# A fused attention and feed-forward kernel: the product of two weights as Strassen's seven products of quarters, with weight tiles in shared places, one-engine copies of G and a new order

## Chip, cores, metric

One core of one Trainium2 chip. The metric is the device time of one execution in microseconds (us). Executions are grouped as fast or slow by the granted TensorE clock and the time, and only fast ones are compared. The chip changes from batch to batch, so every batch carries its own executions of the kernel before. A ratio is the mean time of one kernel's fast runs over the mean of the other's fast runs of the same rounds, so it is not quite the ratio of the medians quoted beside it; the bracket is its 95% interval. The granted clock is the share of TensorE's full rate that the profile shows; a spell at half clock is a stretch in which it was about 0.5. PE is TensorE, DVE VectorE, ACT ScalarE, POOL GpSimd, SP the engine that issues most loads.

## The reference, cut to what matters

```python
def _attn_ref(q, k, v):            # 8 batches, 8 heads, 576 tokens, 64 wide; 32 landmarks
    q_lm, k_lm = (mean of 18 tokens each)
    A, Bm, C = sm(q, k_lm), sm(q_lm, k_lm), sm(q_lm, k)
    Z = (scaled transpose of Bm)
    for _ in range(6):
        Z = 2 * Z - Z @ Bm @ Z
    return A @ Z @ C @ v

def _moe_ref(x, w1, w2, w3, w_out):    # x 4608 x 512; w1, w2 512 x 1024; w3 1024 x 1024; w_out 1024 x 512
    h = (x @ w1) * (x @ w2) @ w3
    return h @ w_out
```

The kernel multiplies the two last weights first: w34 = w3 w_out, in fp32, called **the fold**. It also multiplies the small Z C v with w1 and w2, which gives G, so that x @ w1 becomes A times G.

## The kernel before

A list of tokens gives the order of instructions on all engines. `f` is one product of the fold, `P`, `Q` transposes on PE, `T` a transposing DMA, `M` and `L` token sums (on DVE or POOL), `E` a copy that duplicates a part of w1 and w2 into the other 64 partitions, `G` the part of G from w1 or from w2 for four heads, `U` an up unit, `D` a down chunk, `K` a load of k or q, `W` a load of v, `l` a load of one of the sixteen halves of w3's row blocks. In the new list, `t` transposes such a half, `T1` to `T4` are sums of w_out, and small `g` is a `G` whose copy goes to DVE.

```python
ORDER = """
f f f f f f f f l l f f f l f l f f f f Pk01 f Pk02 Qk00 Qk03 Qq01 f Pq00 l Pk11 f Qk13 f Qq03 Pq02 f
# ... cut ...
U D U U D D D D D
"""

def prod(j, c):                         # the fold: 8 rows x 8 steps of 512 columns, fp32
    if c == 0:
        psw[j] = psf.tile([128, 512], FP32, name="psw", bufs=2)
    nc.tensor.matmul(psw[j], w3ts[j, c // 4][:, c % 4, :], wof[:, c, :],
                     start=(c == 0), stop=(c == 7))
    if c == 7:
        nc.scalar.copy(out=w34[:, j, :], in_=psw.pop(j))

def gproj(b, qd, w):                    # G: 8 matmuls, then one half copied by ACT, one by DVE
    # ... cut ...
    nc.scalar.activation(out=dst[:, 0], in_=psG[:, 0], func=AXF.Copy, scale=1.0 / ZS)
    nc.vector.tensor_scalar(out=dst[:, 1], in0=psG[:, 1], scalar1=1.0 / ZS, scalar2=None,
                            op0=ALU.mult)

def dup_weights(hh):
    nc.vector.tensor_copy(out=wdup[64:128, hh], in_=wdup[0:64, hh])

# the start: SP issues w3, ACT issues w_out in whole rows (five issues)
for i in range(2):
    load_w3(i, nc.sync)
load_wo(0, 1); load_wo(1, 1); load_wo(2, 2)
load_w3(2, nc.sync)
load_wo(4, 2); load_wo(6, 2)
load_w3(3, nc.sync)
```

The softmax here doesn't subtract the row's maximum and nothing guards it: scores larger than these inputs give would overflow.

## Time and profile before

| | before |
|---|---|
| time, median of 3 runs | 298.24 us (296.69 to 299.67) |
| span of the profiled run | 297.0 us, clock 0.987 |
| busy share PE, weight load, DVE, ACT, POOL | 94, 56, 57, 46, 34% |
| first up unit (the first product of ahat and G) starts | 97.2 us |
| from there to the end | 199.8 us |

The prediction below shows the lines of the page. PE is the bound. And the start of the **first up unit** divides the span: nearly all of the fold's work comes ahead of it, and it is the mark. This view of the kernel before gives busy time on both sides of that mark (columns: stretch, length, then PE, weight load, DVE, ACT, POOL busy, granted clock, DMA share, GB/s):

```profile
0.00:97.20 97.20, 91.69 (x921) 48.15 (x922) 48.32 (x106) 32.89 (x59) 36.51 (x57) 1.00 0.98 199
97.20:297.00 199.80, 188.02 (x2772) 118.18 (x2771) 120.17 (x224) 102.52 (x183) 63.38 (x95) 0.98 0.63 125
```

PE is idle 97.2 - 91.69 = 5.5 us ahead of the mark and 199.8 - 188.0 = 11.8 us behind it.

### The profile page before, as it was taken

The page shows a single profiled execution, that of the slowest core. Times are in us where ns is not written, and L with a number is a line of the kernel's source. Part 1 is how long each engine was busy: PE and PEld are TensorE (multiplying, and loading weights), DVE is VectorE, ACT ScalarE, POOL GpSimd, SP SyncE. Part 2 cuts the span into 40 slices and gives each one's busy share as a digit, 9 for nine tenths or more (in the row PEclk, how much of TensorE's full clock was granted, in tenths as well). Part 3 has the DMA queues.
Part 4 walks back from the last instruction along what each step waited for, and adds up shares of the span by engine and source line. Part 5 has one row for each costly group of instructions (what it writes and reads, how often), then busy time and mean ns, then how long its engine had stood idle before and what let it go on. Part 6 is the DMA issues. An engine that isn't in the chain of part 4 may idle for free.

```text
span 297.0 us, 8655 instructions
## 1 busy us (share of the span) xinstructions
PE 279.7 (94%) x3693; PEld 166.3 (56%) x3693; DVE 168.5 (57%) x329; ACT 135.4 (46%) x242; POOL 99.9 (34%) x151
## 2 busy tenths in 40 slices
PE   6999998999998798998899979999999999999994
PEld 2545554555643565675466746635577764566552
DVE  1701587312888868667777576757656466554320
ACT  2015444431144566334666524486565435554341
POOL 0600803640458536386935315381520200000000
PEclk9999999999999999998899998999999999999999
DMA  6999799999979997988988995736931023223234
GB/s 205 376 249 231 192 225 148 178 152 149 155 117 204 235 163 130 169 169 173 216 141 160 142 176 138 110 80 144 256 101 38 4 59 87 71 56 88 67 86 132
DMA packets 57446, 44.34 MB, mean 149 GB/s; under 512 B 30016, under 2 KB 48960, under 8 KB 57408
## 3 DMA queue, kind: packets, MB, share of 16 engines
q1 hardware_dynamic: 42560, 30.06, 45.4%
q0 software_dynamic: 13632, 11.54, 26.2%
q10 hardware_dynamic: 1216, 2.20, 2.1%
q8 instruction: 29, 0.48, 0.7%
q14 instruction: 9, 0.07, 0.1%
HBM read 38.80 MB, written 9.44 MB: 162 GB/s over the span
## 4 chain that ended last, share of the span: by engine, by line
PE 77%; DVE 8%; ACT 7%; DMA 4%; issue 2%; SPq 0%; DVEq 0%; ACTq 0%
PE psw L535 19%; PE small L458 18%; PE big L430 18%; PE small L328 4%; PE big L410 4%; PE small L279 4%; DMA qT<-nat 3%; PE pst L519 2%; PE big L300 2%; ACT gt L414 2%; DVE ab L437 2%; DVE lp L184 2%; ACT a_sb L436 1%; DMA w3f<-in_moe_w_dram 1%; PE small L321 1%
## 5 line engine op out<-in xcount | busy, mean ns | idle before, releaser
L430 PE MATMUL big<-ahat,gt 128*128 128x288 f16 x512 | 73.4, 291 | 4.4 <-DVE gt L415 1.7
L437 DVE TENSOR_TENSOR ab<-a_sb,big 128x576 f16<-128x576 f16 x64 | 48.1, 753 | 37.4 <-ACT a_sb L436 34.3
L458 PE MATMUL small<-w,ab 128*128 128x512 f16 (+1 forms) x296 | 68.0, 376 | 0.1
L535 PE MATMUL psw<-wof,w3t 128*128 128x512 f32 x128 | 64.6, 623 | 0.0
L430 PEld LDWEIGHTS <-gt 128*128 128x128 f16 x512 | 48.8, 99 | 24.9 <-issue 8.8
L436 ACT CAST a_sb<-big 128x576 f16<-128x576 f32 x64 | 40.8, 638 | 25.3 <-PE big L430 23.8
L458 PEld LDWEIGHTS <-ab 128*128 128x128 f16 x296 | 28.2, 99 | 29.8 <-issue 2.7
L462 ACT ACTIVATE o_sb<-small 128x512 f32<-128x512 f32 (+1 forms) x36 | 21.3, 591 | 47.1 <-PE small L458 42.6
L310 POOL TENSOR_TENSOR e<-ect 96x384 f32<-96x384 f32 x16 | 15.9, 996 | 53.9 <-ACT ect L305 51.0
L535 PEld LDWEIGHTS psw<-wof,w3t 128*128 128x128 f32 x128 | 22.0, 195 | 15.1 <-issue 13.6
L415 DVE TENSOR_SCALAR gt<-big 128x512 f16<-128x512 f32 x32 | 21.1, 687 | 10.8 <-ACT gt L414 10.6
L414 ACT ACTIVATE gt<-big 128x512 f16<-128x512 f32 x32 | 18.0, 596 | 9.5 <-PE big L410 9.4
L410 PE MATMUL big<-wdup,zt 128*32 128x512 f16 x256 | 18.5, 397 | 1.9 <-DVE zt L398 1.0
L190 POOL TENSOR_TENSOR ls<-qT 128x384 f32<-128x384 f16 x12 | 11.8, 982 | 24.4 <-ACT qT L134 16.7
L530 ACT COPY w3t<-pst 128x512 f32<-128x512 f32 x13 | 7.6, 586 | 22.1 <-PE pst L519 22.1
L184 DVE TENSOR_REDUCE lp<-kT 128x256 f32<-128x2304 f16 x6 | 15.3, 2548 | 1.3 <-ACT kT L134 1.2
L279 PE MATMUL small<-sz 32*32 32x64 f32 (+1 forms) x768 | 15.0, 215 | 0.6 <-DVE sz L285 0.6
L279 PEld LDWEIGHTS small<-sz 32*32 32x32 f32 x768 | 11.3, 106 | 6.6 <-issue 4.6
L305 ACT ACTIVATE ect<-big 96x768 f32<-96x768 f32 x16 | 12.9, 806 | 4.2 <-PE big L300 4.1
L328 PE MATMUL small<-vt,ect 96*32 96x64 f32 x768 | 13.8, 221 | 0.0
L380 DVE TENSOR_TENSOR ahat<-eat,big 128x576 f16<-128x576 f16 x16 | 11.8, 749 | 3.4 <-PE big L377 3.3
L285 DVE TENSOR_TENSOR sz<-sz,small 128x256 f32<-128x256 f32 x20 | 8.3, 418 | 9.1 <-PE small L279 8.8
(105 smaller groups left out, 296.8 us busy)
## 6 DMA issues: line engine op xcount, KB each, us to landing
vt<-in_v_dram SPq DMA_DIRECT2D x8, 1152.0 KB, 9.4
out_dram<-o_sb SPq DMA_DIRECT2D x23, 192.0 KB, 2.3
nat<-in_k_dram POOLq DMA_DIRECT2D x7, 576.0 KB, 10.9
nat<-in_q_dram POOLq DMA_DIRECT2D x7, 576.0 KB, 8.8
out_dram<-o_sb SPq DMA_DIRECT2D x24, 128.0 KB, 2.4
w3g<-in_moe_w_dram SPq DMA_DIRECT2D x8, 256.0 KB, 6.2
wdup<-in_moe_w_dram POOLq DMA_DIRECT2D x2, 1024.0 KB, 8.8
w3f<-in_moe_w_dram SPq DMA_DIRECT2D x7, 256.0 KB, 6.0
```

The lines of the kernel that those rows point to most:

```text
L184: nc.vector.tensor_reduce(out=lp, in_=tt.rearrange("p h j (l g) -> p h l j g", g=3), axis=AX.XY, op=ALU.add)
L279: nc.tensor.matmul(psI[sl, 64 * a:64 * a + n], src[sl, a, 32:64], src[sl, a, 0:n], start=True, stop=True, tile_position=(32 * h, 32 * h))
L328: nc.tensor.matmul(psV[32 * h:32 * h + 32, 0:64], st["ect", qd][:, c, h, :], st["v"][:, 4 * qd + h, c, :], start=(c == 0), stop=(c == TK - 1),
L410: nc.tensor.matmul(psG[32 * h:32 * h + 32, n, :], st["zt"][h % 2][:, qd, h // 2, :], wdup[:, 4 * qd + h, w, 512 * n:512 * n + 512], start= ...
L414: nc.scalar.activation(out=dst[:, 0], in_=psG[:, 0], func=AXF.Copy, scale=1.0 / ZS)
L415: nc.vector.tensor_scalar(out=dst[:, 1], in0=psG[:, 1], scalar1=1.0 / ZS, scalar2=None, op0=ALU.mult)
L430: nc.tensor.matmul(p[:, c, 0:HS], st["g", qd][:, w, 128 * j:128 * j + 128], st["ahat", qd][:, c, :], start=(qd == 0), stop=(qd == 1))
L436: nc.scalar.copy(out=a_sb, in_=p[:, :, 0:HS])
L437: nc.vector.tensor_tensor(out=ring["ab"][:, j, off:off + S].rearrange("p (c s) -> p c s", c=2), in0=a_sb, in1=pp[1][:, :, 0:HS], op=ALU.mult)
L458: nc.tensor.matmul(pso[:, f0:f1], ab[:, j, pos:pos + 128], w34[:, j, f0:f1], start=(j == 0), stop=(j == 7))
L462: nc.scalar.activation(out=o_sb[:, f0:f1], in_=pso[:, f0:f1], func=AXF.Copy, scale=1.0 / (X64 * X64))
L535: nc.tensor.matmul(psw[j], w3ts[j, c // 4][:, c % 4, :], wof[:, c, :], start=(c == 0), stop=(c == 7))
```

## The change

The intent: the fold's 64 fp32 products of 512 columns become 112 of 256 (Strassen's seven products of quarters, in the form with fifteen sums), which is 12.5% fewer columns for PE. The sums go to DVE and one in each row block to POOL. Of the sixteen halves of w3, fourteen are loaded into the places that w1 and w2 take later and two into a place of G, so no load waits for an earlier half to be used up. One engine copies a whole half of G (ACT 23, DVE 9). Token sums are issued in halves. The order of all work is new, also behind the fold.

```diff
 ORDER = """
-f f f f f f f f l l f f f l f l f f f f Pk01 f Pk02 Qk00 Qk03 Qq01 f Pq00 l Pk11 f Qk13 f Qq03 Pq02 f
+l f f t T1 f l f t T3 l f l l l f t f f f l f l f f t f f T2 f f W1 f T4 f f t f f f f f f f f t f f f f
 ... (all of the list is new)
-    def gproj(b, qd, w):
+    def gproj(b, qd, w, eng):
-        nc.scalar.activation(out=dst[:, 0], in_=psG[:, 0], func=AXF.Copy, scale=1.0 / ZS)
-        nc.vector.tensor_scalar(out=dst[:, 1], in0=psG[:, 1], scalar1=1.0 / ZS, scalar2=None,
-                                op0=ALU.mult)
+        if eng is nc.scalar:
+            nc.scalar.activation(out=dst, in_=src, func=AXF.Copy, scale=1.0 / ZS)
+        else:
+            nc.vector.tensor_scalar(out=dst, in0=src, scalar1=1.0 / ZS, scalar2=None,
+                                    op0=ALU.mult)
+    raws = [wpool.tile([128, 8, 512], FP32, name=f"raw{w}", tag=f"w{w}") for w in range(2)]
+    def wo_sum(i):
+        out, a, b = {1: (T1, B12, B11), 2: (T2, B22, T1), 3: (T3, B22, B12), 4: (T4, B21, T2)}[i]
+        nc.vector.tensor_tensor(out=out, in0=a, in1=b, op=ALU.subtract)
     def turn_w3(i):
+            nc.vector.tensor_tensor(out=s1, in0=pst, in1=tA[r, "22"], op=ALU.add)
+            nc.vector.tensor_tensor(out=s3, in0=tA[r, "11"], in1=pst, op=ALU.subtract)
+            nc.vector.tensor_tensor(out=s2, in0=s1, in1=tA[r, "11"], op=ALU.subtract)
+    PRODS = {1: ("11", B11), 2: ("12", B21), 3: (4, B22), 4: ("22", T4), 5: (1, T1), 6: (2, T2),
+             7: (3, T3)}
+    def prod(r, k, c):
+            acc[r, k] = psf.tile([128, 256], FP32, name="psw", bufs=3)
+        nc.tensor.matmul(ps_, lhs[:, 128 * c:128 * c + 128], right[:, c],
+                         start=(c == 0), stop=(c == 3))
+        elif k == 6:
+            add(tmp[r, "u2"], tmp[r, "p1"])
+            add(tmp[r, "p1"], tmp[r, "u2"], acc[r, 5])
+            nc.gpsimd.tensor_tensor(out=s4, in0=tA[r, "12"], in1=tS[r][2], op=ALU.subtract)
 ... (the other six products add likewise; dup_weights copies two heads at a time; token sums by halves)
-    for i in range(2):
+    for i in range(6):
         load_w3(i, nc.sync)
-    load_wo(0, 1)
-    load_wo(1, 1)
-    load_wo(2, 2)
-    load_w3(2, nc.sync)
-    load_wo(4, 2)
-    load_wo(6, 2)
-    load_w3(3, nc.sync)
+    for c, n, half in ((0, 1, 0), (1, 1, 0), (2, 2, 0), (4, 2, 0), (6, 2, 0), (0, 4, 1),
+                       (4, 4, 1)):
+        load_wo(c, n, half)
```

## The prediction

> **What bounds the kernel now.** I read the page's busy shares first, then the forty slices, the chain of waits, the groups by shape, the PE timeline of the fold (the product of w3 and w_out), and busy time by stretch.
>
> ```profile
> span 297.0 us, 8655 instructions
> PE 279.7 (94%) x3693; PEld 166.3 (56%) x3693; DVE 168.5 (57%) x329; ACT 135.4 (46%) x242; POOL 99.9 (34%) x151
> ...
> PE   6999998999998798998899979999999999999994
> ...
> PE 77%; DVE 8%; ACT 7%; DMA 4%; issue 2%; SPq 0%; DVEq 0%; ACTq 0%
> ```
>
> PE is busy for 94% of the span and carries 77% of the chain; the next engine, DVE, is at 57%. So PE work removed is time removed, as long as no other engine takes the path. PE is idle for 297.0 - 279.7 = 17.3 us. The busy time of each engine by stretch says where:
>
> ```profile
> 0.00:5.00 5.00, 2.69 (x6) 0.76 (x6) 0.78 (x2) 0.00 (x0) 0.70 (x6) 1.00 0.51 176
> 5.00:91.60 86.60, 84.99 (x867) 45.76 (x867) 43.00 (x97) 29.54 (x53) 31.01 (x45) 1.00 1.00 198
> 91.60:98.00 6.40, 4.79 (x56) 2.16 (x55) 5.35 (x9) 3.44 (x7) 5.52 (x8) 1.00 1.05 231
> 98.00:175.00 77.00, 71.07 (x1256) 46.44 (x1255) 54.56 (x106) 41.45 (x73) 39.92 (x60) 0.98 0.96 168
> 175.00:203.00 28.00, 26.38 (x428) 15.30 (x431) 18.42 (x37) 15.62 (x31) 15.10 (x22) 0.94 0.60 111
> 203.00:257.00 54.00, 54.00 (x868) 34.09 (x865) 33.53 (x66) 29.26 (x52) 7.63 (x12) 1.00 0.40 99
> ```
>
> The columns are length, then busy time of PE, weight load, DVE, ACT and POOL, granted clock, DMA share, GB/s. The fold's stretch, 5 to 91.6, has 1.6 us of idle PE; 91.6 to 98 another 1.6; 98 to 203 has 7.6; the rest is start and end. The fold's stretch is therefore bound by PE, with DVE at 43.0 of 86.6 us. What one product costs:
>
> ```profile
> L535 PE MATMUL psw<-wof,w3t 128*128 128x512 f32 x128 | 64.6, 623 | 0.0
> L535 PEld LDWEIGHTS psw<-wof,w3t 128*128 128x128 f32 x128 | 22.0, 195 | 15.1 <-issue 13.6 <-ACT w3t L526 0.5
> ...
> L285 DVE TENSOR_TENSOR sz<-sz,small 128x256 f32<-128x256 f32 x20 | 8.3, 418 | 9.1 <-PE small L279 8.8
> L415 DVE TENSOR_SCALAR gt<-big 128x512 f16<-128x512 f32 x32 | 21.1, 687 | 10.8 <-ACT gt L414 10.6
> L414 ACT ACTIVATE gt<-big 128x512 f16<-128x512 f32 x32 | 18.0, 596 | 9.5 <-PE big L410 9.4
> ```
> ```profile
> 11.91 0.30 PEld L535 LDWEIGHTS psw<-wof,w3t 128*128 128x128 f32 x2
> ...
> 19.77 3.60 PE L535 MATMUL psw<-wof,w3t 128*128 128x512 f32 x8
> 23.20 0.60 PE L519 MATMUL pst<-ident,w3g 128*128 128x128 f32 x4
> 23.64 1.02 PE L535 MATMUL psw<-wof,w3t 128*128 128x512 f32 x2
> ```
>
> There are 64 products but 128 instructions: each fp32 product is two instructions.[...] The pace is (23.20 - 19.77)/8 = 0.429 us. Two weight loads in a row took 0.30 us though one alone lasts 0.19, so the second began about 0.11 after the first[...].
>
> [...]
>
> **The change part by part.**
>
> *PE in the fold.* w3 is cut into 512x512 quarters, w_out into 512x256. Each of four row blocks needs 7 products of 4 steps, so 4 x 7 x 4 = 112 steps of 256 columns in place of 64 of 512. If the pace goes by columns, an instruction takes 0.2145 us, and 224 of them take 48.0 us against 128 x 0.429 = 54.9. That is **6.9 us off**. A weight load (0.11) still fits beneath 0.2145. All sixteen half blocks are still transposed, and nothing of the attention's PE work changes. Switches between the fold and other PE work stay alike: 40 runs of products after, and before 27 plus 14 interruptions by turns, each costing 0.07 to 0.2 us (a pair of instructions is 0.86 undisturbed and 0.93 to 1.06 between others).
>
> *DVE in the fold.* New: 4 sums of 1024 (4.9 us), 3 x 4 sums of 512 (8.3) and 7 x 4 of 256 (11.9): 25 us. Gone there: two exchanges done on DVE (2 x 2.5 us, from copies of 0.29 to 0.31 and sums of 0.42), four of six DVE copies after transposes (1.8), two and a half sums of 2.55 us replaced by seven halves against five wholes (net 3.8), one normalisation (0.75) and a few copies. So 43 + 25 - 12 = 56 us of some 80, about 70%: not the bound, but the products' sums can queue behind a 1.3 us half sum. Hence the sums in halves.
>
> *ACT and POOL in the fold.* ACT loses eight w34 copies (4.7 us) and four turn copies (2.3), and gains 4 small copies, the exchange copies (3.2) and four copies of 0.64: even. POOL gains four sums of 512, some 1.3 us each by the 0.95 us of 384 elements, and two exchanges of 2.2.
>
> *G by one engine.* ACT then DVE takes 0.60 + 0.69 = 1.3 us, one after the other. One ACT copy of 1024 would take about 1.0 us (from 596 at 512 and 806 at 768), one on DVE about 1.2 (687 plus 512 at 1.04 ns). Of 32, 23 go to ACT and 9 to DVE: DVE 21.1 -> 11, ACT 18 -> 23.5. PE waited 2.6 us in all on the DVE half of G, most at 91.6 to 98. Shorter latency and two copies side by side may recover **1 us**.
>
> *Loads.* The w3 halves wait no longer for transposes to free places. By about 16 us PE needs six halves and nearly all of w_out, 3.5 MB, where the trace moved 4.4 MB in its first 15 us. The first k and q tiles now follow 2 MB more of w3, and are needed at 24 to 30 us, much as before. I allow 0.5 us lost here. Turns and attention transposes share one PSUM place instead of two, but the order puts two products (0.86 us) between them, just about a copy of 0.64 with its signal: 0.5 us lost.
>
> *Order.* After the fold, PE idles 1.6 us at 91.6 to 98 and 7.6 until 203. I cannot read a gain out of a list of tokens; I take 0.5 us.
>
> Sum: -6.9 - 1.0 + 0.5 + 0.5 - 0.5 = -7.4; 298.24 - 7.4 = **290.8 us**. The first unit (four products of ahat and g into big) would start near 91 us instead of 97.2.
>
> **The rivals.**
> 1. *The sums become the fold's path.* Every seventh product needs S sums on DVE and one on POOL,[...] a load of k or q issued there waits until its buffer has been transposed (13.0 us once, 5.1 another time), and a sum for the fold behind it holds up PE. For: DVE at 70% and POOL's waits. Against: some five product steps lie between the POOL sum and its use. This would give back 3 to 6 us: 294 to 297.
> 2. *DMA holds the later stages.* The DMA share is 1.00 in the fold and 0.96 until 175 us, k and q go through two buffers, and the chain has a transposing DMA of 8.2 us before 172. A fold that ends 7 us sooner finds the loads no sooner, and the idle PE time of 98 to 203 grows. For: those shares. Against: PE itself is idle only 6 us from 98 to 175,[...] and the new order issues transposes and v earlier. Cost up to 5 us: 292 to 296.
> 3. *The array does not halve.* If an fp32 instruction of 256 columns is paced by its load (0.19 us if not overlapped) or keeps a fixed part of 0.02 us, 4 us of the 6.9 remain: 294.
> 4. *Better all round.* The order also removes half of the later idle time: 286 to 288.
> The granted clock is 0.94 in 175 to 203 and 0.987 on average, about 4 us; one throttled spell more or less moves 2 us either way.
>
> **Range and chances.** The fold's gain is the surest step; rivals 1 and 2 are each worth a third, and rival 4 a fifth. Range 286.5 to 296.5. Faster by over 2% means under 292.3, some 1.5 us above my value: 0.62. Within 2%: 0.35. Slower by over 2% needs two rivals at their worst: 0.03.
>
> **What would show it.** Right: 224 fold instructions at starts 0.21 to 0.22 us apart in undisturbed runs; PE busy near 273 us; the first unit near 91 us; 23 G copies on ACT of 1.0 us and 9 on DVE of 1.2; DVE near 70% in the fold. Wrong: PE waiting for DVE or POOL sums in the fold for over 2 us (rival 1); the stretch from first unit to end longer than the 200 us of now, with waits on transposed k and q (rival 2); pace above 0.23 (rival 3). A span after the first unit below 197 us would show rival 4.

The durations of DVE's sums in it are estimates. What this trace shows for them: a sum of 128x256 took 418 ns, the DVE half of G, 128x512, took 687 ns, and a DVE copy out of PSUM took 292 ns at 128x128 and 693 at 128x512, some 1.04 ns for each further column. From these, 128x512 comes to about 0.69 us and 128x1024 to 1.22, and the new sums to 28 x 0.418 + 12 x 0.69 + 4 x 1.22 = 25 us. In the prediction's table by stretch the DMA share reaches 1.05, so it is not a plain share of time.

## The result

The changed kernel took 286.99 us (median of four runs; 285.25, 292.41 slow, 284.82, 288.72), ratio 0.9603 [0.9496, 0.9711]: faster by 4%, and at the low end of the predicted range or just beyond it. A second submission of the same kernel gave 286.71 us, 0.962 [0.9556, 0.9685]. The page after:

```profile
span 283.5 us, 8897 instructions
...
PE 268.1 (95%) x3789; PEld 183.9 (65%) x3789; DVE 171.8 (61%) x325; ACT 143.4 (51%) x246; POOL 114.0 (40%) x167
```

PE busy fell from 279.7 to 268.1 (near 273 was predicted), and the bound is still PE. The parts that were worked out by durations came as written. The fold's pace, in the PE timeline of the profile after, and the copies of G in its groups:

```profile
24.86 1.89 PE L562 MATMUL psw<-wof,s 128*128 128x256 f32 x8
26.59 0.60 PE L538 MATMUL pst<-ident,raw 128*128 128x128 f32 x4
```
```profile
L418 ACT ACTIVATE gt<-big 128x1024 f16<-128x1024 f32 x23 | 22.8, 1026 | 4.9 <-PE big L412 4.5
```

Eight instructions in 26.59 - 24.86 = 1.73 us, 0.216 us each (0.2145 predicted); G on ACT 1026 ns (1.0 us predicted), nine on DVE 1223 ns (1.2). The view by stretch of the second submission, whose clock was 0.999 (the first one's profiled run was at half clock from 8 to 15 us, so it serves less well):

```profile
0.00:96.70 96.70, 86.76 (x1041) 67.87 (x1042) 64.85 (x131) 35.63 (x64) 49.70 (x71) 1.00 1.05 206
96.70:282.70 186.00, 180.96 (x2753) 115.47 (x2751) 108.54 (x195) 107.61 (x183) 64.72 (x97) 1.00 0.65 131
```

| profiled run, us | before | after (second submission) | difference |
|---|---|---|---|
| to the first up unit | 97.2 | 96.7 | -0.5 |
| of it PE busy / idle | 91.7 / 5.5 | 86.8 / 9.9 | -4.9 / +4.4 |
| from there to the end | 199.8 | 186.0 | -13.8 |
| of it PE busy / idle | 188.0 / 11.8 | 181.0 / 5.0 | -7.1 / -6.7 |

Ahead of the mark, where about 6 us were expected (6.9 of the products, less 1.0 of loads and places), 0.5 came; where 1.5 us were expected, 13.8 came. Of those 13.8, 3.4 us are two spells of 3.41 us at half clock in the run before (139 to 143 and 177 to 180 us), which not every execution has: the nine executions of the kernel before at a clock of 1.0 still took 293.8 to 297.0 us. Some 0.8 us is work that the new order does ahead of the mark (24 matmuls of the k scores at 12 in 0.53 us and 8 of the q scores, 0.3 us, less 8 of G, 0.55 us). 6.7 us is idle time. The other 2.9 us of busy time I cannot attribute. Times below marked **net** have half of each such spell taken off. Net totals are means over the fast executions, with the lost share of the clock taken off, which supposes that PE was at work all through it. Net, the whole gain is some 11 us, from 295.7 to 284.7.

So there are three questions: what ate the fold's gain, what gave the rest, and whether the first can be mended.

### The profile page after: what moved, and what is told of

It reads as the page before. It is cut to its first block, busy times and chain, and to the rows that moved or that the text cites.

```text
span 283.5 us, 8897 instructions
## 1 busy us (share of the span) xinstructions
PE 268.1 (95%) x3789; PEld 183.9 (65%) x3789; DVE 171.8 (61%) x325; ACT 143.4 (51%) x246; POOL 114.0 (40%) x167
## 4 chain that ended last, share of the span: by engine, by line
PE 78%; DVE 8%; ACT 5%; DMA 3%; issue 3%; POOL 1%; SPq 0%; ACTq 0%; DVEq 0%
PE big L433 21%; PE small L461 21%; PE psw L562 14%; PE small L281 5%; PE big L412 4%; PE small L330 4%; PE big L302 2%; DMA raw<-in_moe_w_dram 2%; PE pst L538 2%; PE ptt L136 1%; ACT gt L418 1%; PE big L379 1%; DMA out_dram<-o_sb 1%; DVE wdup L615 1%; PE big L348 1%
## 5 line engine op out<-in xcount | busy, mean ns | idle before, releaser
L433 PE MATMUL big<-ahat,gt 128*128 128x288 f16 x512 | 71.9, 286 | 0.7 <-ACT gt L418 0.4
L418 ACT ACTIVATE gt<-big 128x1024 f16<-128x1024 f32 x23 | 22.8, 1026 | 4.9 <-PE big L412 4.5
L412 PE MATMUL big<-wdup,zt 128*32 128x512 f16 x256 | 17.4, 382 | 0.3 <-ACT gt L418 0.2
L562 PE MATMUL psw<-wof,s 128*128 128x256 f32 x64 | 16.9, 391 | 0.0
L562 PE MATMUL psw<-tmat,s 128*128 128x256 f32 x64 | 16.7, 391 | 0.0
L339 ACT ACTIVATE xd<-small,rcr 128x64 f32<-128x64 f32 x16 | 5.0, 314 | 22.4 <-DVE rcr L337 22.4
L353 ACT ACTIVATE eat<-big 128x576 f16<-128x576 f32 x16 | 10.2, 650 | 8.8 <-PE big L348 8.1
L193 POOL TENSOR_TENSOR ls<-kT 128x384 f32<-128x384 f16 x8 | 7.3, 910 | 16.8 <-DVE kT L137 12.1
L545 ACT COPY a<-pst 128x512 f32<-128x512 f32 x9 | 5.3, 585 | 17.3 <-PE pst L538 14.6
L562 PE MATMUL psw<-wof,a 128*128 128x256 f32 x48 | 13.9, 409 | 0.0
L330 PE MATMUL small<-vt,ect 96*32 96x64 f32 x768 | 13.8, 221 | 0.0
```

The lines of the kernel that those rows point to most:

```text
L330: nc.tensor.matmul(psV[32 * h:32 * h + 32, 0:64], st["ect", qd][:, c, h, :], st["v"][:, 4 * qd + h, c, :], start=(c == 0), stop=(c == TK - 1),
L412: nc.tensor.matmul(psG[32 * h:32 * h + 32, n, :], st["zt"][h % 2][:, qd, h // 2, :], wdup[w][:, 4 * qd + h, 512 * n:512 * n + 512], start= ...
L418: nc.scalar.activation(out=dst, in_=src, func=AXF.Copy, scale=1.0 / ZS)
L433: nc.tensor.matmul(p[:, c, 0:HS], st["g", qd][:, w, 128 * j:128 * j + 128], st["ahat", qd][:, c, :], start=(qd == 0), stop=(qd == 1))
L562: nc.tensor.matmul(ps_, lhs[:, 128 * c:128 * c + 128], right[:, c], start=(c == 0), stop=(c == 3))
```

## The experiments

Eighteen runs followed, in groups on the same chip. My theory was that the fold's gain had been lost at the start and to DVE's copies, and that order and G had made the rest, for which hidden waits for DMA were one possible cause. The rivals: one-engine copies of G alone had made the rest, the order alone had, or the clock had.

**Yardstick.** The change again, unedited.

> The changed kernel once more, as the yardstick on the same chip as the three runs beside it. Expected: 0.955 to 0.965 of the kernel before (285 to 288 us), first unit (first product of ahat and gt) at 95.5 to 97.5 us, PE idle from about 5.3 to 9.8 us and a spell of half clock right after it.

Measured 0.962; it is the second submission above. Its profiled run had no spell of half clock near the start; that part of the expectation was wrong.

### What gave the time behind the first up unit: order and G, in a square

**The change with G copied by two engines** (the old two half copies in `gproj`).

> The changed kernel with G copied as before, half by ACT and then half by DVE. Theory 1 (the copy by one engine gives back the waits on gt after the first unit): 2.5 to 4 us slower than the changed kernel, PE idle on gt up from about 1 us to 3 to 4 us. Rival (the order of the attention work gives them back, and G lies beside other work): within 1 us.

Measured 297.18 us, ratio 0.9989 [0.9933, 1.0044]: the whole gain is gone with this one edit, far more than either side had expected. Some 7 us of it is the edit itself (net 291.5 against 284.7), the rest a lower clock (0.977 to 0.988 in its fast executions).

**The change with the old order behind the fold** (tokens from `X2` on as before, G by one engine), and **the same with G by two engines**.

> The changed kernel up to the end of the fold; after it the tokens in the order of the kernel before (sums in pairs of halves with nothing between, three exchanges on DVE as before). Theory 2 (the new order after the fold removed some 6 us of idle PE and with it the two spells of half clock, 1.7 us each): 7 to 10 us slower than the changed kernel, with PE idle over 0.8 us at least twice after the first unit and at least one spell of half clock after it. Rival (G by one engine or the shorter fold did it): within 2 us of the changed kernel, no such spell.

> The changed kernel with the old order after the fold (the run that took 1.020 of before) and also with G by two engines, as the old order had it. Theory 6 (order and copy were made for each other: the one-engine copy costs time in the old order): faster than the run with the one-engine copy, about 292 to 298 us, 0.985 to 1.0 of before. Rival (the old order loses its time elsewhere, in the sums and exchanges that the new fold's end left undone): as slow as that run or slower, 1.015 or more.

Measured 1.0199 [1.0117, 1.0281], from two fast executions of six, and 1.0175 [1.0117, 1.0233]: slower than the kernel before, fold and all, though not clearly by 2%. The second missed its expectation (0.985 to 1.0): with the new fold, going back to two engines gained only 1.3 us net (299.4 to 298.1), and the intervals overlap.

**The kernel before with G by one engine**, nine of 32 on DVE:

```diff
-        nc.scalar.activation(out=dst[:, 0], ...); nc.vector.tensor_scalar(out=dst[:, 1], ...)
+        if (b, qd, w) not in {(0, 1, 0), (2, 1, 0), ...}:
+            nc.scalar.activation(out=dst, in_=src, func=AXF.Copy, scale=1.0 / ZS)
+        else:
+            nc.vector.tensor_scalar(out=dst, in0=src, scalar1=1.0 / ZS, ...)
```

> The kernel before, its old order and old fold, with G copied whole by one engine (23 by ACT, 9 by DVE, the same ones as in the changed kernel). Theory 1 (the copy by itself is worth most of the 11 us that undoing it cost the changed kernel): 5 to 8 us faster than before. Rival (the copy pays only in the order that was made for it; the old order was made for two engines): within 2 us of before or slower.

Measured 1.0069 [1.002, 1.0119], slightly slower. **The kernel before with each token sum in two halves** (POOL, then DVE, at the old places):

> The kernel before with each sum over tokens done in two halves, one on POOL and then one on DVE, at the places where the whole sums stood; its order, fold and G as before. If the halves by themselves pay (DVE is blocked 1.35 us at a time in place of 2.55, and both engines share each sum): 1 to 3 us faster than before. Rival (they pay only through the new order, which puts other work between the halves): within 1 us of before, or slower.

Measured 1.0396 [1.0312, 1.048]: the halves alone cost 4% (net 302.3 against 296.0), with one wait of 5.0 us for DVE.

Together, net time from the first up unit to the end, from one profiled execution each:

| | G by two engines | G by one engine |
|---|---|---|
| old order behind the fold | 197.7 (with the new fold); 196.4 (before) | 200.7 (with the new fold); 199.0 (before) |
| new order | 191.3 | 186.0 |

One-engine copies cost 2.6 to 3 us in the old order and bring 5.3 in the new one. The order brings 6.4 with two-engine copies and 14.7 with one. The net totals of the new fold agree: the order brings 6.6 us with two-engine copies (298.1 to 291.5) and 14.7 with one (299.4 to 284.7). That one-engine copies cost time in the old order is clear of noise only with the old fold (1.0069). Neither is worth a number of its own; they were tuned for each other. "Order" includes here which engine takes which half sum and which exchange. What the waits are is to be seen in the list of PE's waits from 99 to 203 us (columns: what waited, for what; us in total, times, longest), first of the kernel before, then of the change's second submission, where it is complete:

```profile
PE big L430 <- DVE gt L415: 1.2, 2, 0.9
PE big L430 <- DVE ab L441: 1.2, 1, 1.2
PE big L410 <- DVE zt L398: 1.0, 1, 1.0
PE big L430 <- DVE ab L437: 0.9, 1, 0.9
```
```profile
PE big L433 <- ACT gt L418: 0.4, 1, 0.4
PE big L412 <- ACT gt L418: 0.2, 1, 0.2
```

Before, PE waits for DVE: the half of G, the product ab, zt, and smaller ones; after, 0.6 us in all, none of it DVE. With G by two engines in the new order, 3.5 us of waits for DVE's half of G are back:

```profile
PE big L412 <- DVE gt L417: 3.5, 3, 1.7
```

In the old order one-engine copies turn the waits of 1.6 us for DVE's half of G into 2.9 us for ACT's copy of the whole, and those for ab and zt stay.

**Is it DMA that the order hides?** The kernel before, with v loaded for two batches only and the tiles used again (wrong result, about 7 MB less):

```diff
     def load_v(b):
+        if b > 1:
+            sts[b]["v"] = sts[b % 2]["v"]
+            return
```

> The kernel before, with v loaded for batches 0 and 1 only (wrong result on purpose). If the new order's gain after the first unit, some 10 us, is DMA waits of the old order that the new one hides, the kernel before falls by 4 us or more without v (ratio 0.985 or less) and its idle PE time after the first unit by 4 us. If the old order waits for its engines and not for bytes: within 1.5 us of before, ratio 0.995 to 1.0.

Measured 0.9959 [0.9888, 1.0031], and from the mark to the end 197.1 us against 196.4 net. The old order does not wait for v's bytes. That part of my theory fell; the waits listed are for its engines. (Loads of k and q were not tested so.)

### What ate the fold's gain, first part: the start

ACT timeline of the change, then of the kernel before (columns: start, us, engine):

```profile
4.14 3.81 ACTq L496 DMA_DIRECT2D wof<-in_moe_w_out_dram  x2
7.98 1.28 ACT L543 ACT_TABLE_LOAD   x1 [7.98 <-DMA wof<-in_moe_w_out_dram]
9.27 0.48 ACT L543 COPY a<-pst 128x384 f32<-128x384 f32 x1
```
```profile
5.44 1.28 ACT L526 ACT_TABLE_LOAD   x1 [5.44 <-DMA w3f<-in_moe_w_dram]
6.73 0.48 ACT L526 COPY w3t<-pst 128x384 f32<-128x384 f32 x1
```

ACT itself issues seven loads of w_out instead of five, until 7.95 us. Only then does it load its table and make the first copy of a transposed half, at 9.27 us instead of 6.73. PE stands waiting for it, in the PE timeline after:

```profile
9.80 0.90 PE L538 MATMUL pst<-ident,raw 128*128 128x128 f32 x3 [1.81 <-ACT a L543]
```

**Four of the seven loads issued by SP, between those of w3:**

```diff
-    for i in range(6):
-        load_w3(i, nc.sync)
-    for c, n, half in (...): load_wo(c, n, half)
+    load_w3(0, nc.sync); load_w3(1, nc.sync)
+    for c, n in ((0, 1), (1, 1), (2, 2)):
+        load_wo(c, n, 0)
+    load_w3(2, nc.sync); load_wo(4, 2, 0, nc.sync); load_w3(3, nc.sync); load_wo(6, 2, 0, nc.sync)
+    load_w3(4, nc.sync); load_wo(0, 4, 1, nc.sync); load_w3(5, nc.sync); load_wo(4, 4, 1, nc.sync)
```

> The changed kernel with four of the seven loads of w_out issued by SP between the w3 loads in place of ACT. Theory 3 (the fold's gain was lost at the start: ACT reaches its first copy only at 9.3 us, behind seven issues of loads and the load of its table, PE idles and its clock is halved for 6.8 us after): ACT's first copy at 5 to 6 us, no or a shorter spell of half clock before 16 us, the first unit at 91 to 93 us in place of 96.6 and the whole 3 to 5 us faster than the changed kernel. Rival (the fold is held later by sums, or the later stages by their loads): the first unit no earlier than 95 us, or earlier but the end within 1 us of the changed kernel.

Measured 283.84 us, 0.9497 [0.9428, 0.9566]. Its ACT timeline (the profiled run counts as slow, for a spell at half clock that comes much later, at 83 us):

```profile
2.14 1.28 ACT L543 ACT_TABLE_LOAD   x1 [2.14 <-issue]
5.30 0.48 ACT L543 COPY a<-pst 128x384 f32<-128x384 f32 x1 [1.88 <-PE pst L538]
```

The copy comes 4 us sooner, the fold runs 1.7 us ahead at 29 us, and the kernel gains some 2.8 us (net 281.9 against 284.7; the two intervals just touch, and 3 to 5 us had been expected). So the start is one place where the gain went, worth two fifths of the 6.9.

### What ate it, second part: DVE beside POOL

I had given DVE's sums the durations of an undisturbed engine. Three kinds can be told apart in the fold of the second submission. Sums with one PSUM input kept to the estimate (128x512: 674 to 692 ns; 0.69 us estimated). Sums with both inputs in SBUF did so only when POOL was at rest, or had begun later: s2 took 686, 1000 and 1859 ns, the sums of w_out 1218 to 1966 (1.22 us estimated). Where a sum of w_out at 20.57 us had begun ahead of POOL's sum, it was POOL's that took longer, 2.11 us instead of 1.28. The fp16 duplicating copies took 0.69 us alone and up to 2.14 (the two in the first line below: 2.14 and 1.40). The worst place, DVE, POOL and PE of that run:

```profile
81.67 3.46 DVE L615 COPY wdup<-wdup 64x2048 f16<-64x2048 f16 x2
...
85.89 0.27 DVE L291 TENSOR_TENSOR t<-sz,small 128x128 f32<-128x128 f32 x1
```
```profile
81.11 1.28 POOL L583 TENSOR_TENSOR s<-a,s 128x512 f32<-128x512 f32 x1
82.34 0.91 POOL L193 TENSOR_TENSOR ls<-kT 128x384 f32<-128x384 f16 x1
```
```profile
86.22 0.67 PE L393 MATMUL big<-t,xd 32*64 32x32 f32 x32 [1.38 <-DVE t L291]
```

PE was idle 3.7 us from 70 to 91 us, and this wait is the largest piece. With it the 9.9 us of idle time ahead of the mark are accounted for: 1.7 for ACT's first copy and 1.6 for w3 at the start (before: 0.9 for w3), 1.5 for a first constant as before, 1.4 for this, 1.1 for the small sums of the iteration on DVE, 1.2 without a named cause, and some pieces under 0.6.

**All eight duplicating copies on ACT**, then **two of the eight** (`i in (0, 6)`), both on top of the mended start:

```diff
-        nc.vector.tensor_copy(out=t[64:128, hs], in_=t[0:64, hs])
+        copy = nc.scalar.copy if i in (0, 6) else nc.vector.tensor_copy
+        copy(out=t[64:128, hs], in_=t[0:64, hs])
```

> The kernel with the start mended (SP issues four of the w_out loads), and besides this the copies of wdup into the upper partitions by ACT in place of DVE. Theory 5 (DVE's wdup copies are drawn out while POOL works, up to 1.7 us each where 0.69 is normal, and the sums t and w behind them leave PE idle for 1.3 to 2.3 us near 84 us and more before; ACT is idle there for ten us): idle of PE from 70 to 91 us below 1.5 us in place of 3 to 3.7, and 1.5 to 3 us faster than the kernel with the start alone (0.950 of before), so 0.940 to 0.945. Rival (another wait takes its place): no faster than 0.948.

> The kernel with the start mended, and two of the eight wdup copies (the two that DVE made between 81.7 and 85.1 us, while POOL was at work) by ACT, which is idle there; the six others stay on DVE. (With all eight on ACT the run came to 0.969, slower: PE waited 0.6 and 1.4 us on ACT's copies among the G copies.) Theory 5 (DVE's copies drawn out beside POOL hold up the sum t and with it PE by 1.3 to 2.3 us): PE waits on t under 0.6 us and the whole is 1 to 2 us faster than with the start alone, 0.943 to 0.947. Rival (another wait takes its place): 0.949 or more.

Measured 0.9691 [0.963, 0.9752] for eight, which is too many for ACT, and 0.9497 [0.942, 0.9573] for two: no faster than the mended start alone. Its first up unit came at 93.1 us; with the mended start alone it came at 97.4, of which 3.4 are a spell at half clock, so net at 94.0 (both profiled runs count as slow). **The token of the POOL sum moved instead** (`Lk30` behind `Z0`, copies on DVE):

> The kernel with the start mended, and one half sum on POOL (of batch 3's k) moved from beside those two DVE copies to after the Z product, with nothing else changed. If POOL's work is what draws DVE's copies out (theory 5), the second of the two copies takes under 1 us in place of 1.7, the sum t comes some 1 us sooner, and the run is 0.5 to 1.5 us faster than with the start alone. Rival (the copies are slow for another reason, say the DMA that fills wdup): copies as slow as before, no gain.

```profile
83.26 1.60 DVE L615 COPY wdup<-wdup 64x2048 f16<-64x2048 f16 x2
```

The two copies now took 1.60 us, and the wait behind them 0.26. But the edit is not what did it. Nothing else of POOL's lies between the token's two places, and POOL's sum began at 80.52 us, with the mended start alone at 80.31. What moved was DVE: PE stopped for 2.08 us at 74.78 us, a stop of the kind marked "issue" that is treated below, and the two copies came at 83.26 us, when POOL was nearly done, instead of at 78.74, where they had taken 4.36 us. Another copy, 0.69 us long at 76.68 before, now fell beside POOL's sum at 80.36 and took 1.63. The kernel was not faster: 0.9599 [0.9544, 0.9655], where the mended start alone had 0.9497. What speaks for POOL is all the profiles together: of 142 such copies in the twenty, 63 had no TENSOR_TENSOR of POOL beside them and took 677 to 690 ns, and each of those over 0.71 us (the longest 3065 ns) had one beside it for 0.34 us or more. No run takes POOL's work away alone, so this is a regularity, not an experiment.

### Strassen against 64 products in the same frame

**The change with the classic fold** of 64 products of 512 columns, all else alike:

> The changed kernel with its loads, turns, places, new order and one-engine G, but the fold as 64 products of 512 columns as before, spread evenly over the 112 places of the order; no sums on DVE or POOL for it, w34 copied by ACT. Theory 4 (the seven products save what their PE time says, 6.9 us): the first unit 6 to 8 us later than the 96.7 of the changed kernel and the whole 5 to 8 us slower. Rival (in this order the fold's stretch is held by DVE and its sums, so that fewer sums make up for more products): within 2 us of the changed kernel.

Measured 0.9971 [0.9907, 1.0035], but the run was unfair: w_out still came in column halves, so the classic products waited 6.30 us for it at the start. Mended with w_out in whole rows and five issues on ACT:

> The run with 64 products of 512 columns in the new order once more, with w_out now loaded in whole rows by five issues as in the kernel before. (In the first such run PE sat idle for 6.3 us at the start until the right half of w_out had come, which is no fault of the 64 products.) Theory 4 (the seven products save about 6 us of PE time in the fold): 4 to 6 us slower than the changed kernel, so 0.975 to 0.985 of before, first unit at 98 to 102 us. Rival (nothing is left of it once the start is fair): 0.967 or less. Either way it is faster than before by what the new order and the copy by one engine do after the fold.

Measured 288.69 us, 0.9731 [0.9674, 0.9787], net 288.4, with the first up unit at 98.8 us. Against the change (0.962, net 284.7, on another chip) Strassen as built is worth 3.6 us, about 1.1%, half of the 6.9; the intervals overlap a little. But this run, with its five issues, has its first copy on ACT at 6.82 us and the change at 9 us. Against the version with the mended start (5.30 us; 0.9497, net 281.9) the difference is 6.5 us, clear of noise: with a fair start on both sides, nearly all of the 6.9 is there.

### An earlier fold, and one execution that ended no earlier

In the profiles the version with two copies on ACT is 3.6 us ahead of the change at the first up unit, and 0.8 us behind it at 139 us. Its profiled run counts as slow, with a clock of 0.998, and its fast executions keep the lead (net 281.3 against 284.7). So what follows explains that one execution, not the kernel. Its chain of waits (start, us, what) in between:

```profile
102.30 14.67 DMA qT<-nat
117.04 0.52 issue
117.56 0.79 POOL nat L99
...
132.18 0.32 ACT xd L339
132.54 1.89 PE small L461 x8
```

A transposing DMA took 14.67 us from issue to landing, and behind it came POOL's load, four blocks of POOL sums, and xd (the small product C v), which PE waited for. That wait is 1.3 of the 4.3 us for which PE was idle from 99 to 140 us; 2.5 us are three stops marked "issue", treated below, and have no known tie to the DMA. The SP queue of the same run shows what went out just ahead of it:

```profile
97.00 0.91 SPq L112 DMA_DIRECT2D vt<-in_v_dram  x1
102.30 7.99 SPq L120 DMA_TRANSPOSE qT<-nat  x1
```

**That version without the later loads of v** (wrong, edit as above), and **the change likewise**:

> a_start with two duplicating copies on ACT, and v loaded for batches 0 and 1 only (the old tiles used again, so the result is wrong on purpose; 7 MB of 21 MB less of v and its queue). Theory (what gives the earlier end of the fold back after the first unit is DMA: k and q queue behind v and w): span after the first unit falls from 190.4 us to 186 us or less, the transposed k and q of batch 2 come at least 3 us earlier against the start, total 280 us or less (ratio 0.94). Rival (it is given back by POOL's sums and the chain of small steps, not by bytes): total stays within 1 us of the same kernel with v, 284 us, ratio 0.95.

> The change, with v loaded for batches 0 and 1 only (wrong result on purpose). Theory (DMA hides what the fold gains, and less in the change itself since its fold ends later): 1 to 3 us under the change, ratio 0.955. Rival (no bytes matter): same, 0.962 within 0.004.

Measured 281.34 us, 0.9471 [0.9395, 0.9546]; the time behind the mark fell from 190.4 to 185.8 us, and idle PE time from 99 to 140 us from 4.3 to 0.9 us. The total I had asked for, 280 us, was missed by 1.3. That run had no stop marked "issue" from 99 to 140 us either. In time it is no clear gain: with v, the two submissions gave 0.9497 [0.942, 0.9573] and 0.9578 [0.9485, 0.9672]. For the change itself v's bytes do not matter: 0.9627 [0.9557, 0.9697], as the rival had it. So a wait behind a transposing DMA appears in a trace with an earlier fold, and not in the change; that it costs the kernel time is not shown.

**One load moved, with the right result.** The load of v of batch 3 goes out behind the transposing DMA of q of batch 4 (`s_w3`); besides, that of batch 2 ahead of the transposing DMA of k of batch 3 (`s_w23`); and the version without either on the same chip:

```diff
-N11 Kq4 A21 Mk31 C20 N01 G011 Mq30 C21 U U Tk4 A20 U Mq31 G110 W3 U Tq4 X3 v20 ...
+N11 Kq4 A21 Mk31 C20 N01 G011 Mq30 C21 U U Tk4 A20 U Mq31 G110 U Tq4 W3 X3 v20 ...
```

> Yardstick on the same chip: the kernel with SP issuing four w_out loads and two duplicating copies on ACT. Both theories: ratio 0.950 as before, first unit near 93 us, 190 us from there to the end.

> The same with one token moved: the load of v of batch 3 is issued behind the transposing DMA of q of batch 4, not ahead of it. Theory (that load's bytes held the transposing DMA up for 14.7 us from 102.3 us, and so the chain of POOL's sums, lx and xd): the DMA of q lands some 5 us after its issue, the wait of 1.3 us on xd and the idle PE time of 99 to 140 us (4.3 us) fall to about 1 us, 2 to 3 us in all, ratio 0.942. Rival (the giving back is POOL and the order, any queue with v in it costs the same): ratio 0.950 within 0.003, idle PE time of 99 to 140 us 3.5 us or more.

> The same with, besides, the load of v of batch 2 ahead of the transposing DMA of k of batch 3, within the fold. Theory (only v's place against the transposes of 93 to 103 us matters): as s_w3 or up to 1 us better, ratio 0.940. Rival: the load now holds up the transposes of 70 to 83 us instead and a wait appears there: ratio 0.950 or more.

Measured on one chip: 0.9578 [0.9485, 0.9672] for the yardstick, **0.9508 [0.9441, 0.9575] (280.82 us)** with one load moved, 0.9711 [0.9624, 0.9797] with two. The yardstick had few fast runs; one of its four executions ran at half clock for 427 of 436 us (438 us in all) and is left out, as is a slow one. Its SP queue, with one load moved:

```profile
98.44 3.64 SPq L120 DMA_TRANSPOSE qT<-nat  x1
102.14 0.57 SPq L112 DMA_DIRECT2D vt<-in_v_dram  x1
```

The transposing DMA is through the queue in 3.6 us, idle PE time of 99 to 140 us is 1.3 us as expected, and the wait for xd is gone. The ratio I had expected, 0.942, was missed, since the yardstick itself stood at 0.958 and not 0.950 on this chip; the step between them, 0.7%, is of the expected size, though the two intervals overlap. The second edit made it worse, and not as either side had it. The first up unit came at 100.6 us, 8.9 later than with one load moved, yet PE waited for no transposed k or q. Its timeline shows where the time went:

```profile
73.87 0.31 PE L348 MATMUL big<-qT,lmk 64*32 64x288 f16 x7 [1.89 <-issue]
...
85.50 1.01 PE L330 MATMUL small<-vt,ect 96*32 96x64 f32 x26 [2.00 <-issue]
```

Two stops without a named cause, 3.9 us, and two spells at half clock after them of 3.41 and 6.83 us, which cost half of that, 5.1 us: together about the 8.9. Net of the clock its fast executions are 3.3 us above those with one load moved (284.3 against 281.0), near the 3.9 of the stops. My theory had this wrong; the rival had the ratio right (0.950 or more) but not the cause.

The version with one load moved has its first up unit at 91.7 us, the place that the prediction had named for the change (near 91), and 187.3 us from there. Three of its four executions took 280.5 to 280.8 us. Its median is the lowest with a right result, 0.951 of the kernel before on its chip. By ratio it is no better than the mended start alone (0.9497), so what came after that edit is not shown to have paid.

### Stops marked "issue"

Such stops are in many of the profiles: PE halts in the middle of a group of equal matmuls, waiting for nothing that the profile names, in eight profiles at the matmul of the first line above, at 74 to 78 us, else at one of a few other places. The page counts packets of a DMA queue of kind "instruction": 30 in the change, each of 16,384 bytes in its trace, for 2 x 3789 = 7578 instructions on PE, one packet for 253; 29 in the kernel before, for 2 x 3693 = 7386, one for 255. In thirteen of the twenty profiles there are 20 such stops between 60 and 150 us, and in 19 of them PE goes on 0.94 to 1.53 us after such a packet has landed (once 2.28); in the change's first profile three packets landed at 66.18, 75.56 and 126.87 us and PE went on at 67.54, 76.72 and 128.25. In five profiles of the seven products, at full clock there, without the stop at this matmul the packet had gone out at 65.6 to 68.8 us; in the eight with it, at 70.9 to 75.3. So these stops, 0.3 to 2.3 us each, may be PE waiting for its own next instructions; that these packets bring them is read from the name of the kind and the counts alone. This is a coincidence in 19 of 20 cases, not an experiment: no run delays such a packet alone, and why one goes out late is open.

## Why the prediction was wrong where it was

The number, 290.8, was 4 us high. Two steps failed, in opposite directions: the fold's gain did not reach the first up unit, and G and order, counted at 1.5 us, brought about 10 together. The second is why the kernel came out faster than forecast. Step by step:

- **"If the pace goes by columns ... 6.9 us off"; "the first unit ... near 91 us".** This step failed. The pace was right (0.216). PE busy time ahead of the first up unit fell by 4.9 us with some 0.8 us of other work moved ahead of it, so near 6. But idle time there grew by 4.4 us, and the first up unit came 0.5 us sooner, not 6. In the same frame Strassen was worth 3.6 us, and 6.5 with the start mended.
- **Loads, "I allow 0.5 us lost here".** Mis-sized, and mostly in the wrong place: PE waited 1.6 us for w3 at the start (0.9 before), but more was lost by the issuing. ACT issues seven loads before its first copy, which comes 2.5 us later than before. Mended, the kernel gains about 2.8 us.
- **"DVE in the fold ... about 70%: not the bound"; rival 1.** The share was right (64.9 of 96.7 us, 67%; by the prediction's own sums 48.3 + 25 - 12 = 61.3 us up to the mark), and it was not POOL's queue that held PE up. But the estimates of 0.69 and 1.22 us held only for sums with a PSUM input (674 to 692 ns) or with POOL at rest (686; 1226 and 1228); beside POOL, the copies and sums with both inputs in SBUF took up to three times as long (2.14 us for 0.69). A wait of 1.4 us for DVE followed. Rival 1 is right in part, in this other form.
- **"G by one engine ... 1 us" and "Order ... 0.5 us".** This step failed too: durations right, worth wrong. Together they made about 10 us net behind the first up unit (196.4 to 186.0, of which 0.8 is work moved ahead of it). They are not terms of a sum: one-engine copies cost 2.6 us in the old order and bring 5.3 in the new. Before, "PE waited 2.6 us in all on the DVE half of G" was read rightly, but the other waits on DVE (ab, zt) were left with "I cannot read a gain out of a list of tokens".
- **Rival 4**, "a span after the first unit below 197 us", is what happened, at 186. I gave it a fifth. It should have had more, since the list of idle PE time, 11.8 us behind the mark, was larger than all the work to be taken from the fold.
- **Rival 2** was not at work in the change as far as v goes (0.9627 without its loads). With an earlier fold one profile shows it, as a wait of 1.3 us.
- **Rival 3** did not happen.

The total came within 1.5% because two errors of opposite sign met: some 6 us lost in the fold and some 9 us more found behind it.

## What to carry to other kernels

When a change removes work from the bounding engine, follow one mark near the end of that stage, not the total: here busy time there fell by 4.9 us while idle time took 4.4 back, and another part of the change paid. Do not count on the undisturbed duration of DVE operations with two SBUF inputs, or of fp16 copies within SBUF, where POOL is at work (here 0.69 us without POOL's sums, and up to 1.86 for a sum of 128x512 and 3.07 for a copy of 64x2048 beside them), and count what the copying engine must issue before its first copy (here seven loads until 7.95 us). And try an order and the split of work between engines together, in a square of four runs: here one-engine copies cost time in the old order and gained most in the new one.

## What stays open

- What sets the granted clock to half. In the run before, two spells of 3.41 us followed stretches whose longest idle gap was 0.96 and 1.20 us; gaps of 1.2 to 1.7 us in the change's second submission had none after them.
- What a large load just ahead costs a transposing DMA. The chain shows 14.67 us with a load of 1152 KB issued 5.3 us before it, and with that load moved behind, the same transpose left the queue after 3.64 us instead of 7.99. In the change's first submission such a load went out 0.7 us ahead, and the transpose left the queue after 7.32 us and landed after 11.0.
